# ScalarE instead of VectorE for the residual sums of three feed-forward units

## The chip, the cores and the metric

The program runs on one core of a Trainium2 chip. The metric is the device time in microseconds (us) of one execution. TensorE is PE in the profile's tables, its weight loads are PEld, VectorE is DVE, ScalarE is ACT, GpSimd is POOL, and SP is the queue from which nearly all transfers are issued.

## What is computed

Two layers over 2048 tokens of width 640, in float32. Each layer is a sliding-window attention (32 heads of 20, eight keys two tokens apart) behind a layer norm, and a feed-forward of width 1536 behind two layer norms, each with a residual sum:

```
def _B_ref(x, w1, b1, w2, b2):
    y = _layernorm(x, axis=-1)
    h = _gelu(jnp.einsum("bsd,df->bsf", y, w1) + b1)
    return jnp.einsum("bsf,fd->bsd", h, w2) + b2

x = A_x
x = x + _A_ref(_layernorm(x, axis=-1), A_wqkv, A_wo)
x = x + _B_ref(_layernorm(x, axis=-1), B_w1, B_b1, B_w2, B_b2)
x = x + _A_ref(_layernorm(x, axis=-1), A_wqkv, A_wo)
x = x + _B_ref(_layernorm(x, axis=-1), B_w1, B_b1, B_w2, B_b2)
return x
```

The last line of `_B_ref` together with its caller is the sum that the change moves: x + b2 + h·w2.

## The kernel before, in words

The tokens are cut into four sets of 512 (four tiles of 128 tokens), and each set passes both layers, so there are eight units: 0 to 3 are the first layer, 4 to 7 the second. The residual stream x stays in SBUF for the whole run (the tile is called xf). Products are made from float16 pairs: every operand is split into a high and a low half, and three of the four half products are summed (`PASS`). Weights carry a factor WS = 64, which is taken out at the end of each sum.

A unit has five steps. (1) Layer norm, then a transposing DMA writes the transposed halves into a yT buffer (L619). (2) The query, key and value products, called QKV below (L647), are copied out of PSUM by ScalarE (L664) and spilled to DRAM, and the windows come back into the tiles qk and v. (3) Attention is nearly all VectorE: products with the queries (L731), sums over a head (L735), the soft maximum, products with the values (L757), sums over the window (L765, L769). It runs in 32 groups, four to a unit. The split of its result (L776, L779) is transposed by DMA (L792). (4) The output projection, called WO below (L804): ScalarE first writes 64·x into the PSUM bank (L816), TensorE adds its products to it without a start flag, and ScalarE copies the sum back to x divided by 64 (L821). (5) Two layer norms and the feed-forward.

The feed-forward of a unit is `mlp`. For each of twelve blocks e of 128 hidden columns there is an inner product (L859, 15 matmuls of 512 columns into one of three banks "ps"), a gelu (L865) and the copy of its high half (L868) on ScalarE, the low half on VectorE (L870), and the outer products (L880), which add up over all twelve blocks in five PSUM banks. Banks acc0 to acc3 (acc_97 to acc_100 in the orders below) hold the first 512 columns of the four tiles, and acc4 (acc_101) holds the last 128 columns of all four. The block's first weights go through three buffers c1 (c_78 to c_80), its second weights through three buffers c2 (c_81 to c_83), each loaded again from DRAM for every block of every unit (L852). GpSimd adds b2 to x ahead of time (L624), and at the unit's end five VectorE additions (from L903 and L908, through the helper at L915) add the five banks, divided by 64, to x. Unit 0 is done in two halves. Units 6 and 7 are done together by another function, `pair` (L1052, L1087 and others), which takes over the same banks and is not touched.

The order of the work is not the order of this code. Every instruction, or small group of them, is handed to a planner (`class Plan`) as an operation with an estimated duration, a priority, what it needs, what it gives and which buffers it uses. The planner simulates the five engines and the DMA queue, picks on each engine the ready operation of lowest priority number, and so fixes the order on every engine. Each engine then runs its list strictly in that order. A different operation in one place can therefore reorder everything planned after it, on every engine and in the SP queue.

Of the kernel before, what the change touches and what calls it, by code (L numbers as in the profile page):

```python
# [18 lines left out]
NF = F // P  # L19
# [4 lines left out]
WS = 64.0  # L24
# [7 lines left out]
M = 4  # L32
# [33 lines left out]
PAIRS = ("qk", "pv", "ad", "o", "sub", "at", "hlo", "yl", "xb", "ol", "wq", "lo", "lm")  # L66

TURN = 2.7

THROUGH = (("sa", 29),)  # L70
LOP = ((29, -460),)
# [218 lines left out]
def sliding_dilated_then_mlp_kernel(  # L290
# [138 lines left out]
    def mm(cols, n, prio, emit, need=(), give=(), use=()):  # L429
        plan.add("pe", cols / 2400.0 + 0.0028 * n, prio, emit, need, give, use)  # L430
# [398 lines left out]
    def mlp(at, b, t0, t1):  # L829
# [8 lines left out]
        def bank(i):  # L838
            return (f"acc{i}", at)

        def own(i):
            return i, 0, 0, BANK

        def rest(i):
            return M, i * REST, BANK, REST

        for e in range(NF):
            j = at * NF + e
            pk, hk, h32 = ("ps", ("in", j)), ("hh", j), ("h32", j)
# [25 lines left out]
            def outer(i, passes, pieces, wk=wk, hk=hk, e=e, seen=seen):  # L875
                for a, c in passes:
                    for k, c0, w0, n in pieces:
                        first = e == 0 and k not in seen
                        seen.add(k)
                        nc.tensor.matmul(accs[k][:, c0:c0 + n], tile_of(*hk)[:, a, (i - t0) * P:(i - t0 + 1) * P],  # L880
                                         tile_of(*wk)[:, c, w0:w0 + n], start=first,
                                         stop=e == NF - 1 and (a, c) == PASS[-1], skip_group_check=True)

            if e < NF - 1:
                for i in tiles:
                    prev = [("outh", b, e - 1, i)] if e else ([("outh", b, e, i - 1)] if i > t0 else [])
                    mm(2 * D, 4, j, lambda i=i, outer=outer: outer(i, PASS[:2], [own(i), rest(i)]), need=[("hhi", j), wk, *prev],
                       give=[("outh", b, e, i)], use=[wk, hk, bank(i), last])
                    mm(D, 2, j + 0.05, lambda i=i, outer=outer: outer(i, PASS[2:], [own(i), rest(i)]),
                       need=[("hlo", j), ("outh", b, e, i)], give=[("out", b, e, i)], use=[wk, hk, bank(i), last])  # L890
# [6 lines left out]
        for i in tiles:  # L897
# [5 lines left out]
        dve(REST * (t1 - t0), -991, lambda: add(  # L903
            x[u][:, t0:t1, BANK:], accs[M][:, t0 * REST:t1 * REST].rearrange("p (t c) -> p t c", c=REST)),
            need=[("out", b, NF - 1, ("rest", at)), *[("xb", b, i) for i in tiles]], give=[("xr", la + 1, u, i) for i in tiles],
            use=[last])
        for i in tiles:
            dve(BANK, -990, lambda i=i: add(x[u][:, i, :BANK], accs[i]),  # L908
                need=[("out", b, NF - 1, i), ("xb", b, i)], give=[("x", la + 1, u, i)], use=[bank(i)])
            if la == 1:  # L910
                dma(P * D * 4 / 1e3, -900, lambda i=i: nc.sync.dma_start(rows(out, u)[:, i], x[u][:, i]),
                    need=[("x", la + 1, u, i), ("xr", la + 1, u, i)], give=[("done", u, i)])

    def add(xs, ps, plus=None):
        nc.vector.scalar_tensor_tensor(xs, ps, 1.0 / WS, xs if plus is None else plus, op0=OP.mult, op1=OP.add)  # L915
# [411 lines left out]
```

## Time and profile before

| | us |
|---|---|
| three runs | 1149.23, 1156.69, 1147.42 |
| their median | 1149.23 |
| profiled execution, its own time | 1146.92 |
| its span, first to last instruction | 1145.1 |
| what lies around the span | 1.8 |
| TensorE busy in the span | 1136.8 |
| VectorE busy | 1052.4 |
| ScalarE busy | 594.2 |
| GpSimd busy | 113.9 |

The profile is one execution. "Busy" counts the time in which an engine has an instruction under way; matmuls overlap each other, so the mean time of one is longer than the step from one to the next, and the step is busy time over count where they run back to back. The page's groups give line, engine, operation, tiles out<-in, shapes and count, then busy us, mean ns, and the idle time just before them with what ended it. A timeline row gives start, duration, engine, line, operation, tiles, shape and count of merged instructions.

### The profile page before, as it was taken

How to read it: one execution, taken by the hardware profiler on the slowest of the kernel's cores; microseconds unless marked ns; L12 is line 12 of the kernel's file. 1: busy time of each engine (PE TensorE's matmuls, PEld its weight loads, DVE VectorE, ACT ScalarE, POOL GpSimd, SP SyncE). 2: the span in 40 equal slices, each digit the busy share in tenths (PEclk: the TensorE clock that was granted, in tenths of full speed). 3: DMA queues.
4: the chain of work that ended last, by engine and by line, in shares of the span. 5: the costliest groups of instructions: out<-in, count | busy, mean ns of one | idle time of the engine just before them, and what ended most of it. 6: DMA issues, size and time to landing. Idle time of an engine off the chain costs nothing.

```text
span 1145.1 us, 17492 instructions
## 1 busy us (share of the span) xinstructions
PE 1136.8 (99%) x6834; PEld 629.1 (55%) x6834; DVE 1052.4 (92%) x1043; ACT 594.2 (52%) x1103; POOL 113.9 (10%) x94
## 2 busy tenths in 40 slices
PE   9999999999999999999999999999999999999998
PEld 6444446576655465546555645555455555554476
DVE  7899999999999999999999999999999995858972
ACT  6385436636355276725627653378257334747630
POOL 1010000111101111120112011012110000000000
PEclk9999999999999999999999999999999999999999
DMA  9999999988786478567755775577666656885101
GB/s 304 307 296 269 303 347 251 300 290 243 224 247 193 132 217 220 166 200 202 187 201 181 194 180 193 179 189 196 184 201 172 202 176 162 183 251 150 43 24 69
DMA packets 239790, 235.47 MB, mean 206 GB/s; under 512 B 139020, under 2 KB 195164, under 8 KB 239708
## 3 DMA queue, kind: packets, MB, share of 16 engines
q1 hardware_dynamic: 239708, 234.36, 69.8%
q8 instruction: 53, 0.87, 0.3%
q14 instruction: 29, 0.24, 0.1%
HBM read 157.55 MB, written 44.78 MB: 177 GB/s over the span
## 4 chain that ended last, share of the span: by engine, by line
PE 89%; DVE 6%; issue 2%; DMA 2%; ACT 1%; POOL 0%; SPq 0%; POOLq 0%; DVEq 0%; ACTq 0%
PE ps L647 31%; PE acc L880 19%; PE ps L859 18%; PE ps L804 10%; PE acc L1052 4%; PE ps L1087 4%; PE ps L1052 2%; DVE pr L757 1%; DVE pr L731 1%; DVE pr L765 1%; DMA qk<-spill 1%; PE acc L1087 1%; DMA c<-mw 1%; DVE pr L984 1%; PE acc L1248 1%
## 5 line engine op out<-in xcount | busy, mean ns | idle before, releaser
L647 PE MATMUL ps<-wq,yT 128*128 128x480 f16 (+1 forms) x1950 | 391.0, 363 | 0.5 <-DMA yT<-w 0.2
L647 PEld LDWEIGHTS <-yT 128*128 128x128 f16 x1950 | 189.3, 98 | 199.1 <-DMA yT<-w 0.5
L880 PE MATMUL acc<-c,act 128*128 128x512 f16 (+1 forms) x1728 | 249.1, 299 | 0.0
L859 PE MATMUL ps<-yT,c 128*128 128x512 f16 (+1 forms) x1260 | 246.6, 349 | 1.3 <-DMA c<-mw 1.3
L880 PEld LDWEIGHTS <-act 128*128 128x128 f16 x1728 | 136.1, 98 | 106.6 <-issue 0.2
L731 DVE TENSOR_TENSOR pr<-qk 128x2560 f32<-128x2560 f32 x64 | 181.2, 2835 | 3.1 <-DMA qk<-spill 3.1
L735 DVE TENSOR_REDUCE sm<-pr 128x128 f32<-128x2560 f32 x64 | 179.4, 2806 | 0.2
L757 DVE TENSOR_TENSOR pr<-sm,v 128x2560 f32<-128x2560 f32 x64 | 179.0, 2818 | 0.4
L859 PEld LDWEIGHTS <-c 128*128 128x128 f16 x1260 | 120.2, 98 | 107.5 <-DMA c<-mw 1.6
L664 ACT ACTIVATE ev<-ps 128x480 f32<-128x480 f32 x128 | 72.4, 566 | 169.4 <-PE ps L647 155.3
L765 DVE TENSOR_TENSOR pr<-pr 128x640 f32<-128x640 f32 (+1 forms) x128 | 144.6, 1160 | 0.2
L804 PE MATMUL ps<-wo,yT 128*128 128x320 f16 x960 | 131.9, 299 | 0.0
L865 ACT ACTIVATE act<-ps,b 128x512 f32<-128x512 f32 (+1 forms) x84 | 52.3, 623 | 151.0 <-PE ps L859 141.1
L804 PEld LDWEIGHTS <-yT 128*128 128x128 f16 x960 | 93.9, 98 | 37.7 <-issue 0.2
L779 POOL TENSOR_TENSOR ohl<-w,ohl 128x640 f16<-128x640 f32 x24 | 34.3, 1431 | 472.6 <-DVE pr L731 346.8
L870 DVE TENSOR_TENSOR act<-act 128x512 f16<-128x512 f32 (+1 forms) x84 | 51.4, 614 | 10.3 <-ACT act L868 10.0
L586 POOL TENSOR_TENSOR ln<-ln,half 128x2 f32<-128x2 f32 (+1 forms) x31 | 34.7, 1125 | 225.6 <-ACT ln L583 225.5
L624 POOL TENSOR_TENSOR xf<-xf,b 128x640 f32<-128x640 f32 x24 | 39.9, 1663 | 151.8 <-DVE ohl L779 47.9
L569 ACT ACTIVATE junk<-xf 128x640 f16<-128x640 f32 x57 | 41.8, 733 | 15.6 <-DVE xf L813 8.0
L609 ACT ACTIVATE w<-xf,ln 128x640 f32<-128x640 f32 x53 | 47.1, 909 | 2.6 <-DVE w L617 2.5
L868 ACT ACTIVATE act<-act 128x512 f16<-128x512 f32 (+1 forms) x84 | 47.4, 566 | 1.8
L776 ACT ACTIVATE ohl<-w 128x640 f16<-128x640 f32 x32 | 23.5, 735 | 46.7 <-DVE w L769 46.1
(196 smaller groups left out, 1002.9 us busy)
## 6 DMA issues: line engine op xcount, KB each, us to landing
c<-mw SPq DMA_DIRECT2D x174, 320.0 KB, 3.6
spill<-ev SPq DMA_DIRECT2D x64, 480.0 KB, 3.5
qk<-spill SPq DMA_DIRECT2D x32, 880.0 KB, 5.8
v<-spill SPq DMA_DIRECT2D x32, 880.0 KB, 5.2
qk<-spill SPq DMA_DIRECT2D x32, 320.0 KB, 3.7
act<-in_B_w_dram SPq DMA_DIRECT2D x24, 320.0 KB, 5.4
mw<-c SPq DMA_DIRECT2D x24, 320.0 KB, 5.3
pr<-in_B_w_dram SPq DMA_DIRECT2D x24, 320.0 KB, 4.1
```

The costliest lines, as they stand in the source:

```text
L647: nc.tensor.matmul(ps, transposed(yk)[:, a * KD + k, t * P:(t + 1) * P], wq[:, b, k, g, i0:i1], start=first and j == 0, stop=last and j == ...
L664: act(3 * GC, -400 + n, lambda i=i, pk=pk, ek=ek: nc.scalar.activation(tile_of(*ek)[:, :, i], tile_of(*pk)[:, :3 * GC].rearrange("p (a c) ...
L731: nc.vector.tensor_mul(tile_of(*pk), w[:, HALO + m + t0:HALO + m + t0 + EH, None, :].to_broadcast([P, EH, W, GC]), windows(w, t0, [GC, W], ...
L735: dve(E, G - 0.7, lambda pk=pk, t0=t0: nc.vector.tensor_reduce(lg(t0, t0 + EH).rearrange("p t w h -> p (t w h)"), tile_of(*pk).rearrange(" ...
L757: nc.vector.tensor_mul(tile_of(*vk).rearrange("p t w (h d) -> p t (w h) d", d=DH), lg(t0, t0 + EH).rearrange("p t w h -> p t (w h)")[:, :, ...
L765: dve(EH * w * GC, G - 0.9, lambda vk=vk, w=w: nc.vector.tensor_add(tile_of(*vk)[:, :, 0:w], tile_of(*vk)[:, :, 0:w], tile_of(*vk)[:, :, w ...
L804: nc.tensor.matmul(tile_of(*pk)[:, :D // 2], transposed(yk)[:, a * KD + k, t * P:(t + 1) * P], wo[:, b, k, c * D // 2:(c + 1) * D // 2], s ...
L859: nc.tensor.matmul(tile_of(*pk)[:, :nt], tile_of(*ck)[:, a, k * P:(k + 1) * P], transposed(yk)[:, c * KD + k, t0 * P:t1 * P], start=i == 0 ...
L865: act(nt, -430, lambda pk=pk, h32=h32, e=e: nc.scalar.activation(tile_of(*h32)[:, :nt], tile_of(*pk)[:, :nt], AF.Gelu_apprx_tanh, bias=b1[ ...
L880: nc.tensor.matmul(accs[k][:, c0:c0 + n], tile_of(*hk)[:, a, (i - t0) * P:(i - t0 + 1) * P], tile_of(*wk)[:, c, w0:w0 + n], start=first, s ...
L1052: nc.tensor.matmul(tile_of(*to(i))[:, :HALF], hl()[:, a, i * P:(i + 1) * P], row(c), start=start and (a, c) == PASS[0], stop=(a, c) == PAS ...
L1087: nc.tensor.matmul(ps, wt()[:, a, w0:w0 + P], z(c), start=start and k == 0, stop=k == 3 * len(todo) - 1, skip_group_check=True)
```

## The change

For units 3, 4 and 5 (`filled = b > 2`) the five VectorE additions at the unit's end are gone. In their place ScalarE does ten things. Before the unit's first outer product it writes 64·(x + b2) into the five banks ("fills": four of 128x512, one of 128x4x128 for acc4), and the outer products then add to this with no start flag on any of them. After the last outer product ScalarE copies the five banks, divided by 64, back to x ("drains"). The first outer products (e = 0) of each tile need the fill of that tile's bank and that of acc4; the fill of acc4 comes last and needs x + b2 of all four tiles. The fill of a bank needs the bank free, which is after the drain of the unit before. Units 0 to 2 keep the VectorE additions, and units 6 and 7 are not touched.

```diff
+FILL, DRAIN = -420, -700
...
+        filled = b > 2
+        put = [("put2", b, i) for i in tiles] + [("put2", b, "rest")] if filled else []
+
+        if filled:
+            for i in tiles:
+                act(BANK, FILL, lambda i=i: nc.scalar.activation(accs[i], x[u][:, i, :BANK], AF.Copy, scale=WS),
+                    need=[("xb", b, i)] + [("out", b - 1, NF - 1, i)] * (b > 0), give=[("put2", b, i)], use=[bank(i)])
+            act(REST * M, FILL, lambda: nc.scalar.activation(
+                accs[M].rearrange("p (t c) -> p t c", c=REST), x[u][:, :, BANK:], AF.Copy, scale=WS),
+                need=[("xb", b, i) for i in tiles] + [("out", b - 1, NF - 1, ("rest", at - 1))], give=[("put2", b, "rest")], use=[last])
...
-                        first = e == 0 and k not in seen
+                        first = not filled and e == 0 and k not in seen
...
-                    mm(2 * D, 4, j, lambda i=i, outer=outer: outer(i, PASS[:2], [own(i), rest(i)]), need=[("hhi", j), wk, *prev],
+                    mm(2 * D, 4, j, lambda i=i, outer=outer: outer(i, PASS[:2], [own(i), rest(i)]), need=[("hhi", j), wk, *prev] + [("put2", b, i), ("put2", b, "rest")] * (filled and e == 0),
...
+        if filled:
+            act(REST * M, DRAIN, lambda: nc.scalar.activation(
+                x[u][:, :, BANK:], accs[M].rearrange("p (t c) -> p t c", c=REST), AF.Copy, scale=1.0 / WS),
+                need=[("out", b, NF - 1, ("rest", at))], give=[("xr", la + 1, u, i) for i in tiles], use=[last])
+        else:
+            dve(REST * (t1 - t0), -991, lambda: add(
...
         for i in tiles:
+            if filled:
+                act(BANK, DRAIN, lambda i=i: nc.scalar.activation(x[u][:, i, :BANK], accs[i], AF.Copy, scale=1.0 / WS),
+                    need=[("out", b, NF - 1, i)], give=[("x", la + 1, u, i)], use=[bank(i)])
+            else:
+                dve(BANK, -990, lambda i=i: add(x[u][:, i, :BANK], accs[i]),
+                    need=[("out", b, NF - 1, i), ("xb", b, i)], give=[("x", la + 1, u, i)], use=[bank(i)])
```

The new lines shift the line numbers: behind the top of the file by 1, from the inner products on by 12, and from `add` on by 21. So L865 before is L877 now, L804 is L805, L1087 is L1108.

The planner's order is the same on every engine up to the start of unit 3's outer products, and different after it. Ahead of the first outer products of unit 3 TensorE now has three inner products in a row where it had one. Ahead of those of units 4 and 5 it has two where it had one. Three places follow.

The first place is ScalarE's list where unit 3 ends and unit 4 begins. The rows are gelus of inner products (L865, act<-ps), copies of their high halves (L868, act<-act) and layer norm steps (L569, L573). Before:

```order
L865 ACTIVATE act<-ps_94,b_104 128x512
L868 ACTIVATE act<-act 128x512
L569 ACTIVATE junk,ln_93<-xf 128x640 x2
L573 ACTIVATE junk,ln_93<-xf,ln_93 128x640 x2
L569 ACTIVATE junk,ln_93<-xf 128x640
L865 ACTIVATE act<-ps_95,b_104 128x512
```

And now the same place, with the drains (xf<-acc) and the fills (acc<-xf):

```order
L877 ACTIVATE act<-ps_94,b_104 128x512
L916 ACTIVATE xf<-acc_101 128x4x128
L880 ACTIVATE act<-act 128x512
L926 ACTIVATE xf<-acc_97 128x512
L926 ACTIVATE xf<-acc_98 128x512
L926 ACTIVATE xf<-acc_99 128x512
L926 ACTIVATE xf<-acc_100 128x512
L853 ACTIVATE acc_97<-xf 128x512
L853 ACTIVATE acc_98<-xf 128x512
L853 ACTIVATE acc_99<-xf 128x512
L853 ACTIVATE acc_100<-xf 128x512
L855 ACTIVATE acc_101<-xf 128x512
```

Five drains and five fills now stand between two gelus, and the layer norm that reads the new x stands behind the fills instead of behind VectorE's additions.

The second place is the SP queue a little later, before the output projection of unit 5. c<-mw rows load feed-forward weights, yT<-ohl rows are the transposes that the projection reads, yT<-w rows those of a layer norm. Before:

```order
L852 DMA c_81<-mw_126 128x1280
L689 DMA v_68<-spill_138 128x1760
L792 DMA_TRANSPOSE yT_72<-ohl_75 128x10x128 x4
L619 DMA_TRANSPOSE yT_74<-w_86 128x10x128
L619 DMA_TRANSPOSE yT_74<-w_85 128x10x128
```

And now:

```order
L690 DMA v_68<-spill_138 128x1760
L864 DMA c_78<-mw_117 128x1280
L864 DMA c_81<-mw_126 128x1280
L864 DMA c_82<-mw_127 128x1280
L793 DMA_TRANSPOSE yT_72<-ohl_75 128x10x128 x4
```

The four transposes now stand behind the load into c_82, whose buffer comes free only when the second of two blocks of outer products of unit 4 is done.

The third place is TensorE's list at the output projection of unit 7. Before, at this row an inner product (L859) is followed by a block of outer products (L880):

```order
L859 LDWEIGHTS c_80
L859 MATMUL ps_96<-yT_72,c_80 128x512
L880 LDWEIGHTS act
L880 MATMUL acc_97<-c_81,act 128x512
L880 MATMUL acc_101<-c_81,act 128x128
```

And now, at the same row, the inner product is followed by the output projection:

```order
L871 LDWEIGHTS c_80
L871 MATMUL ps_94<-yT_72,c_80 128x512
L805 LDWEIGHTS yT_73
L805 MATMUL ps_95<-wo,yT_73 128x320
```

The projection of unit 7 has moved ahead by one block of outer products and one inner product.

More of the change, by code (lines that the diff above doesn't have):

```diff
@@ L901, in mlp @@
                need=[("hlo", j), ("outh", b, e, i)], give=[("out", b, e, i)], use=[wk, hk, bank(i)])
[L903 to L906, printed above, removed]
-        for i in tiles:
-            dve(BANK, -990, lambda i=i: add(x[u][:, i, :BANK], accs[i]),
-                need=[("out", b, NF - 1, i), ("xb", b, i)], give=[("x", la + 1, u, i)], use=[bank(i)])
+        if filled:
[4 more added lines that the diff above has]
+            dve(REST * (t1 - t0), -991, lambda: add(
+                x[u][:, t0:t1, BANK:], accs[M][:, t0 * REST:t1 * REST].rearrange("p (t c) -> p t c", c=REST)),
+                need=[("out", b, NF - 1, ("rest", at)), *[("xb", b, i) for i in tiles]], give=[("xr", la + 1, u, i) for i in tiles],
+                use=[last])
+        for i in tiles:
+            if filled:
[4 more added lines that the diff above has]
+                    need=[("out", b, NF - 1, i), ("xb", b, i)], give=[("x", la + 1, u, i)], use=[bank(i)])
             if la == 1:
```

## The prediction

> **What bounds the kernel now.** I read the engines' busy shares first, then TensorE's own waits, then its step per matmul, then stretches of time around and behind the change.
>
> ```profile
> PE 1136.8 (99%) x6834; PEld 629.1 (55%) x6834; DVE 1052.4 (92%) x1043; ACT 594.2 (52%) x1103; POOL 113.9 (10%) x94
> ...
> PE ps L1087 <- ACT xf L1156: 1.6, 1, 1.6
> PE acc L1248 <- POOL ident L446: 1.4, 1, 1.4
> PE ps L859 <- DMA c<-mw: 1.3, 1, 1.3
> PE ps L647 <- DMA yT<-w: 0.2, 1, 0.2
> PE acc L1052 <- ACT act L1059: 0.2, 1, 0.2
> ```
>
> TensorE is idle for 1145.1 − 1136.8 = 8.3 us of the whole span, and its five named waits are 4.7 us together. A busy TensorE need not be a fast one, so I check the step from one matmul to the next, which is busy over count where they run back to back:
>
> ```profile
> L647 PE MATMUL ps<-wq,yT 128*128 128x480 f16 x1905 | 387.7, 366 | 0.3 <-DMA yT<-w 0.2
> L804 PE MATMUL ps<-wo,yT 128*128 128x320 f16 x960 | 131.9, 299 | 0.0
> ...
> 750.40 3.42 PE L880 MATMUL acc<-c,act 128*128 128x128 f16 x24
> 753.66 3.40 PE L859 MATMUL ps<-yT,c 128*128 128x512 f16 x15
> 756.90 3.42 PE L880 MATMUL acc<-c,act 128*128 128x512 f16 x24
> 760.16 2.11 PE L859 MATMUL ps<-yT,c 128*128 128x512 f16 x9
> ```
>
> 387.7/1905 is 203.5 ns for 480 columns, 131.9/960 is 137.4 ns for 320: 0.424 and 0.429 ns a column. The timeline gives the feed-forward: a block of 24 outer matmuls (12 of 512 and 12 of 128 columns) takes 3.26 us from its start to the next one's, and 15 inner matmuls 3.24 us, both for 7680 columns: 0.424 and 0.422 ns. Four shapes have one price per column, so there are no gaps hidden in the busy time. The columns are fixed by the arithmetic, and the change leaves their number as it is.
>
> ```profile
> 600.00:1010.00 410.00, 409.97 (x2446) 219.99 (x2445) 383.75 (x355) 218.96 (x404) 47.52 (x32) 1.00 0.67 187
> 1010.00:1090.00 80.00, 78.14 (x408) 39.49 (x406) 63.42 (x104) 52.27 (x83) 0.00 (x0) 1.00 0.43 129
> 1090.00:1145.10 55.10, 51.75 (x381) 37.05 (x379) 26.60 (x54) 8.96 (x15) 0.00 (x0) 1.00 0.14 48
> ```
>
> The columns after the stretch are TensorE, its weight loads, VectorE, ScalarE and GpSimd busy, then the granted clock (1.00 throughout), DMA share and GB/s. The change begins at 610 us. From there to 1010 us TensorE has no idle time at all, between 1010 and 1090 us it has 1.86 us, and 3.35 us lie at the very end, where the last sums are added and sent, in a function that is not touched. VectorE is nearly full up to 930 us, but nobody waits for it in TensorE's list: the planner fills each of its delays with feed-forward blocks of an earlier unit.
>
> **The change part by part.** *VectorE's additions go.*
>
> ```profile
> L915 DVE SCALAR_TENSOR_TENSOR xf<-acc,xf 128x512 f32<-128x512 f32 x29 | 18.4, 682 | 1.4 <-PE acc L880 1.4
> ```
>
> A step is 18.4/29 = 0.63 us, and 15 of them are 9.5 us of VectorE: 3.2 us by 760 us, 6.3 us by 920 us, the rest at unit 5's end. None of it lies on TensorE's path, so its worth is slack for VectorE and 0 us by itself.
>
> *ScalarE's drains and fills come.* There are 30. The nearest rows are copies of 512 columns from PSUM to SBUF, and the fill of the output projection at 320 columns; the gelu and its copy, which stand between them, follow:
>
> ```profile
> L1156 ACT ACTIVATE xf<-ps 128x512 f32<-128x512 f32 x6 | 3.5, 581 | 0.0
> L1159 ACT ACTIVATE wq<-ps 128x512 f32<-128x512 f32 x4 | 2.4, 592 | 2.5 <-PE ps L1087 2.4
> L816 ACT ACTIVATE ps<-xf 128x320 f32<-128x320 f32 x56 | 23.6, 432 | 0.5
> L865 ACT ACTIVATE act<-ps,b 128x512 f32<-128x512 f32 x60 | 41.1, 684 | 123.0 <-PE ps L859 117.5 <-DVE pr L765 5.1
> L868 ACT ACTIVATE act<-act 128x512 f16<-128x512 f32 x60 | 37.6, 626 | 1.2
> ```
>
> At 0.59 us each, 30 are 17.7 us on an engine that is busy for half of the time. What counts is the chain at each unit's start. At units 4 and 5 TensorE's last outer block ends with the last tile (at 753.66 in the rows above), then two inner blocks follow, 2 × 3.24 = 6.5 us, and e = 0 starts at 760.1. In between ScalarE has at least the last drain and five fills, 6 × 0.59 = 3.5 us, and at most all ten, 5.9 us. Both fit, with 0.6 to 3.0 us to spare. With one inner block, as the order was, even the shorter chain would not have fitted into 3.24 us; the second inner block is the cover, and if it were gone the price would be 0.3 to 2.7 us a unit.
>
> At unit 3 VectorE still adds unit 2's sums, and the fills wait for them and for the last x + b2 on GpSimd:
>
> ```profile
> 610.98 3.08 DVE L915 SCALAR_TENSOR_TENSOR xf<-acc,xf 128x512 f32<-128x512 f32 x5
> ...
> 611.14 1.54 POOL L624 TENSOR_TENSOR xf<-xf,b 128x640 f32<-128x640 f32 x1 [4.40 <-DVE act L870]
> ...
> 610.79 3.40 PE L859 MATMUL ps<-yT,c 128*128 128x512 f16 x15
> ```
>
> The last addition ends at 614.06 and the last b2 at 612.68. Were the whole list of five fills, one layer norm row (0.74, below), one gelu and its copy (1.3) to run only from 614.06 on, the acc4 fill would end at 614.06 + 3.0 + 2.0 = 619.1. Three inner blocks hold TensorE until 610.79 + 3 × 3.24 = 620.5. It fits with 1.4 us at worst. The drains at unit 5's end stand before the pair's products into the same banks; the rows of inner products between them cover about 2 us, and I price this at 0 to 1 us, taking 0.
>
> *Waits behind the new work.* ScalarE's list is strict, so gelus and layer norms stand behind the ten. Only unit 3's sums are read by another layer (units 4 and 5 are outputs).
>
> ```profile
> 753.31 0.74 ACT L569 ACTIVATE junk<-xf 128x640 f16<-128x640 f32 x1 [1.36 <-DVE xf L915]
> ...
> 772.01 4.53 SPq L619 DMA_TRANSPOSE yT<-w  x3
> ...
> 786.38 3.81 PE L647 MATMUL ps<-wq,yT 128*128 128x480 f16 x18
> ```
>
> That layer norm began at 753.31 and now begins behind the fills, at 757.2 or later, some 4 us. Its transposes, issued from 772.0 on, move to 776, and the QKV products move back by one outer block to 789.6. The margin shrinks from 14.4 to about 13.6 us: 0. In the SP queue the transposes for unit 5's projection now wait for the second outer block of unit 4, which ends at 760.1 + 6.5 = 766.7. The projection begins at 773.2, one outer block after the row before (769.9), and a transpose lands 3.4 to 7.3 us after its issue, in the middle 4.3:
>
> ```profile
> 769.89 16.65 PE L804 MATMUL ps<-wo,yT 128*128 128x320 f16 x120
> DMA to landing us min/median/max: 3.4/4.3/7.3
> ```
>
> That is 771.0 for the first tile, 774.0 at the latest: 0 to 0.8 us, and I take 0.
>
> The tightest place is unit 7's projection. It moves ahead by one outer and one inner block, 6.5 us, from 961.7 to 955.2:
>
> ```profile
> 953.08 0.82 DVE L779 TENSOR_TENSOR ohl<-w,ohl 128x640 f16<-128x640 f32 x1 [0.80 <-ACT ohl L776]
> ...
> 954.51 9.06 SPq L792 DMA_TRANSPOSE yT<-ohl  x4
> ...
> 955.24 3.42 PE L880 MATMUL acc<-c,act 128*128 128x512 f16 x24
> 958.50 3.40 PE L859 MATMUL ps<-yT,c 128*128 128x512 f16 x15
> 961.74 4.51 PE L804 MATMUL ps<-wo,yT 128*128 128x320 f16 x32
> ```
>
> Its transposes were issued at 954.5, 7.2 us ahead. VectorE is to be 6.3 us earlier there, so issue comes at 948.2, 7.0 us ahead. If VectorE's relief arrives in full the wait is 0 to 0.3 us; if none of it arrives, 6.5 us.
>
> ```profile
> 630.00:780.00 150.00, 150.00 (x883) 80.57 (x882) 148.18 (x124) 81.17 (x152) 17.84 (x12) 1.00 0.71 189
> 780.00:850.00 70.00, 69.97 (x380) 36.02 (x379) 69.24 (x56) 31.22 (x64) 13.39 (x8) 1.00 0.68 191
> 850.00:930.00 80.00, 80.00 (x502) 43.78 (x500) 79.01 (x66) 41.26 (x73) 4.11 (x4) 1.00 0.60 185
> ```
>
> VectorE idles for 3.6 us in these 300 us, so a shorter list ends earlier by nearly as much; I take 0.5, near the first end.
>
> *The tail.* The pair's order is new too. Before, it holds one wait of 1.6 us for ScalarE's L1156 and 1.86 us idle in all. The new order may lose it or hold others: −1.9 to +2 us, and I take −0.5, since the pair's layer norm comes earlier.
>
> The sum is 0 + 0 + 0.5 − 0.5 = 0: a span of 1145.1 us and, with the 1.8 us around it, 1146.9 us for the execution, rounded to 1147. The median of the runs shown, 1149.2, stands 2.3 us above that execution.
>
> **The rivals.** *Unit 7's projection waits.* VectorE's relief is eaten by the layer norm's low halves, which now come later from ScalarE. The price is up to 6.5 us, typically 4 with the tail: 1151. For it speaks the small margin, against it that VectorE is full and takes any work early.
>
> *The fills become the bound (slower).* If ScalarE reaches the drains late in each filled unit, because an Exp with its two table loads stands in the chain, the outer products of e = 0 wait:
>
> ```profile
> L746 ACT ACT_TABLE_LOAD x20 | 25.7, 1283 | 0.4
> L746 ACT ACTIVATE sm<-sm 128x256 f32<-128x256 f32 x32 | 13.3, 415 | 27.9 <-DVE sm L744 27.6
> ```
>
> The Exp and a table load on either side of it are 3 us, and with a gelu and copy (1.3 us) a chain of 5.9 grows to 10.2, against a cover of 6.5: 3.7 us a unit, 11 us for three, and 1158. It decides from a chain of 10.3 us on. Against it: the order has the Exp behind the fills.
>
> *VectorE is the true bound (faster).* If its additions delayed attention one for one up to the end, 9.5 us would go: 1137. VectorE's 92% speaks for it, the 410 us without a gap in TensorE against it. The Trainium skill, Perfetto Trace Analysis, section Identifying the Most-Contended Engine, holds matmul busy time a poor measure of headroom and names weight-load busy time instead; by that rule TensorE stands at 55%, VectorE is the most-contended engine, and the time would be the 1137 of this rival. This trace disagrees: the constant 0.42 to 0.43 ns a column shows a full TensorE.
>
> **How the numbers follow.** About 1% (11.5 us) is what a measurement of this kernel can tell from no change. My forecast, no more than 4 us from 1147, gets 0.74; the late projection 0.12; the fills as the bound 0.09, of which 0.08 lie beyond 1%; VectorE as the bound 0.05, of which 0.02 lie beyond it. So: faster by over 1% 0.02, within 1% 0.90, slower 0.08. The range goes from 1142 (the tail's 1.9 us gone and a quick execution) to 1154 (the late projection at its full 6.5 us); it leaves out the fills, VectorE and the ends of the others, some 0.17.
>
> **What would show it.** Right: TensorE still without idle time between 600 and 1010 us, VectorE's busy time 9.5 us less, ScalarE's some 16 more, L853 and L855 done before e = 0 starts, WO of unit 7 near 955 us. Wrong: an idle time of TensorE before L892 that a fill ends (the fills), before L805 that a transpose ends (unit 7), new waits of L1108, or a span shorter by more than 4 us, which would mean that TensorE's busy time was not its floor.

## The result, and the profile after

The changed kernel takes 1146.16 us (median of 22 runs, 1144.6 to 1147.8), the kernel before 1149.97 us (22 runs, 1146.7 to 1161.0). The ratio is 0.9956, interval 0.994 to 0.9972: the same by the prediction's measure of 1%, and 3.8 us less in the median. The forecast was 1147.0 in a range of 1142 to 1154. Three executions of this record ran at a granted clock of 0.26 to 0.85 (4321.6, 2018.0 and 1322.5 us) and stand in no median or count below. The two profiled executions differ by much less than the medians: 1146.3 us with a span of 1144.5, against 1146.92 with 1145.1. So most of the gain is not to be found by laying those two traces side by side. What changed most is the spread: in the kernel before six of 22 executions lay above 1155, in the changed one none lies above 1148.

The page after, its first line, and TensorE's waits (engine, tile, line, what it waited for: us in all, times, longest):

```profile
PE 1136.8 (99%) x6834; PEld 629.0 (55%) x6834; DVE 1041.5 (91%) x1028; ACT 609.3 (53%) x1133; POOL 115.3 (10%) x94
...
PE acc L1269 <- POOL ident L447: 1.3, 1, 1.3
PE acc L892 <- DVE xf L936: 1.3, 1, 1.3
PE ps L648 <- ACT xf L822: 0.9, 1, 0.9
PE ps L1108 <- DVE wq L1182: 0.3, 1, 0.3
PE ps L648 <- DMA yT<-w: 0.2, 1, 0.2
```

TensorE's busy time is the same to the tenth, VectorE has 10.9 us less, ScalarE 15.1 us more. Gone is the wait of 1.6 us for L1156 at the pair's start; new are the third line and, with 0.3 us, the fourth. (The second line, at 266 to 268 us, lies ahead of the change.) The three stretches of the prediction, columns as there:

```profile
600.00:1010.00 410.00, 409.09 (x2436) 219.01 (x2434) 378.06 (x350) 234.38 (x433) 49.41 (x32) 1.00 0.67 189
1010.00:1090.00 80.00, 79.66 (x426) 40.94 (x424) 60.10 (x99) 53.98 (x88) 0.00 (x0) 1.00 0.40 120
1090.00:1144.50 54.50, 51.13 (x377) 36.55 (x374) 24.79 (x51) 6.56 (x11) 0.00 (x0) 1.00 0.14 49
```

TensorE loses 0.9 us in the stretch of the change, where it lost nothing, and gains 1.5 us in the pair (0.34 idle, 1.86 before). That accounts for the 0.6 between the two executions. The places on which the prediction rested, from the timeline after (start, duration, engine and line):

```profile
756.81 0.59 ACT L855 ACTIVATE acc<-xf 128x512 f32<-128x512 f32 x1
...
760.51 6.68 PE L892 MATMUL acc<-c,act 128*128 128x512 f16 x48
...
773.53 2.74 PE L805 MATMUL ps<-wo,yT 128*128 128x320 f16 x19
...
948.82 8.92 SPq L793 DMA_TRANSPOSE yT<-ohl  x4
...
956.50 5.73 PE L805 MATMUL ps<-wo,yT 128*128 128x320 f16 x41
```

Unit 4's last fill ends at 757.4, 3.1 us before e = 0 needs it. The projections of units 5 and 7 begin at 773.5 and 956.5 and wait for nothing.

The new wait of 0.9 us is small, but it holds the key to the rest. This is what the engines do ahead of it, in the timeline after:

```profile
779.24 5.54 DVE L758 TENSOR_TENSOR pr<-sm,v 128x2560 f32<-128x2560 f32 x2
784.71 0.81 DVE L618 TENSOR_TENSOR w<-w,w 128x640 f16<-128x640 f32 x1
785.45 2.88 DVE L766 TENSOR_TENSOR pr<-pr 128x1280 f32<-128x1280 f32 x2
791.51 0.82 DVE L618 TENSOR_TENSOR w<-w,w 128x640 f16<-128x640 f32 x1 [3.19 <-ACT w L616]
...
782.27 7.32 POOL L780 TENSOR_TENSOR ohl<-w,ohl 128x640 f16<-128x640 f32 x1 [12.17 <-ACT w L616]
...
789.62 0.92 ACT L610 ACTIVATE w<-xf,ln 128x640 f32<-128x640 f32 x1 [4.00 <-POOL ohl L780]
790.44 0.41 ACT L822 ACTIVATE xf<-ps 128x320 f32<-128x320 f32 x1
790.91 9.27 PE L648 MATMUL ps<-wq,yT 128*128 128x480 f16 x45 [0.91 <-ACT xf L822]
```

GpSimd's subtraction L780 takes 1.4 us elsewhere in this trace. Here it takes 7.3. VectorE goes from one operation with two inputs in SBUF straight to the next, from 779.2 to 788.3, and GpSimd's ends 1.3 us after that row does. ScalarE's list is strict: its L610 needs the buffer that L780 reads, waits 4.0 us for it, and behind L610 stands the copy that frees a PSUM bank for TensorE. So VectorE can hold TensorE up without TensorE ever waiting for VectorE by name: through GpSimd, which is busy for 10% of the time, and ScalarE's list.

The Trainium skill, SBUF — State Buffer, section Who interferes with whom, says that a VectorE instruction with two SBUF inputs contends with a GpSimd instruction that reads SBUF, that the contention is an exclusive lock, and that the order of issue decides who blocks. This trace agrees: VectorE's row began first, and GpSimd's operation took 7.3 us against 1.4.

### The profile page after: what moved, and what is told of

The parts are those of the page before. It is cut to its first block, busy times and chain, and to the rows that moved or that the text cites. A ratio compares the mean times of both kernels' runs of the same rounds, so it can differ in the third digit from the quotient of the medians.

```text
span 1144.5 us, 17537 instructions
## 1 busy us (share of the span) xinstructions
PE 1136.8 (99%) x6834; PEld 629.0 (55%) x6834; DVE 1041.5 (91%) x1028; ACT 609.3 (53%) x1133; POOL 115.3 (10%) x94
## 4 chain that ended last, share of the span: by engine, by line
PE 91%; DVE 5%; issue 1%; ACT 1%; POOL 1%; DMA 0%; DVEq 0%; POOLq 0%; ACTq 0%
PE ps L648 34%; PE ps L871 19%; PE acc L892 19%; PE ps L805 10%; PE acc L1073 3%; PE ps L1108 3%; PE ps L1073 2%; DVE pr L1005 1%; POOL ohl L780 1%; PE acc L1269 1%; DVE pr L758 0%; DVE pr L732 0%; DVE sm L736 0%; DMA yT<-w 0%; DVE pr L766 0%
## 5 line engine op out<-in xcount | busy, mean ns | idle before, releaser
L805 PE MATMUL ps<-wo,yT 128*128 128x320 f16 x960 | 131.7, 299 | 0.0
L877 ACT ACTIVATE act<-ps,b 128x512 f32<-128x512 f32 (+1 forms) x84 | 52.3, 622 | 129.4 <-PE ps L871 125.0
L805 PEld LDWEIGHTS <-yT 128*128 128x128 f16 x960 | 93.7, 98 | 37.4
L780 POOL TENSOR_TENSOR ohl<-w,ohl 128x640 f16<-128x640 f32 x24 | 39.9, 1664 | 466.5 <-DVE pr L732 274.9
L625 POOL TENSOR_TENSOR xf<-xf,b 128x640 f32<-128x640 f32 x24 | 37.4, 1559 | 147.5 <-DVE ohl L780 44.9
L610 ACT ACTIVATE w<-xf,ln 128x640 f32<-128x640 f32 x53 | 47.5, 910 | 7.3 <-POOL ohl L780 4.0
L618 DVE TENSOR_TENSOR w<-w,w 128x640 f16<-128x640 f32 x56 | 44.9, 817 | 4.6 <-ACT w L616 4.4
L880 ACT ACTIVATE act<-act 128x512 f16<-128x512 f32 (+1 forms) x84 | 47.3, 565 | 3.3 <-PE acc L892 1.5
```

Source lines behind the costliest of these rows:

```text
L805: nc.tensor.matmul(tile_of(*pk)[:, :D // 2], transposed(yk)[:, a * KD + k, t * P:(t + 1) * P], wo[:, b, k, c * D // 2:(c + 1) * D // 2], s ...
L877: act(nt, -430, lambda pk=pk, h32=h32, e=e: nc.scalar.activation(tile_of(*h32)[:, :nt], tile_of(*pk)[:, :nt], AF.Gelu_apprx_tanh, bias=b1[ ...
```

## Experiments

The first four runs were made before the place just shown was understood; their theories are "relief" (VectorE's shorter list removes the spread), "order" (the new order does), "tail" (the pair's wait) and "late inputs" (what VectorE makes for the output projections comes just in time). From the fifth run on the theory is the lock: GpSimd's small operations wait for VectorE's rows, and ScalarE and then TensorE wait for them. Its rival is late inputs: a longer VectorE list reaches TensorE by itself.

**1. The kernel before, profiled again.** No edit.

> The kernel before, unchanged, once more with a profile: its runs scatter from 1146.7 to 1161.0 us, those after the change only from 1144.6 to 1147.8, and the profile of before was a quick execution. If the late-input theory holds (the inputs that VectorE makes for the output projections come just in time), an execution of 1150 us or more shows 3 us or more of idle TensorE before L804 at units 5 to 7, near 770, 848 or 962 us. If the tail theory holds (the pair's new order), the idle time lies in L1087 or L1052 after 1010 us. If it lies before 610 us, neither holds, since both kernels have the same order there.

Measured: 1149.26 us, span 1147.5; the 25 executions of before beside it fall into two groups, 18 from 1146.9 to 1150.8 and 7 from 1153.9 to 1155.8. This profile is 2.4 us longer than the first one of the same kernel. The timelines of the two at one place, the first profile of before and then this one:

```profile
789.37 3.98 POOL L624 TENSOR_TENSOR xf<-xf,b 128x640 f32<-128x640 f32 x1 [5.33 <-DVE pr L765]
793.32 1.28 POOL L586 TENSOR_TENSOR ln<-ln,half 128x2 f32<-128x2 f32 x1
```

```profile
789.75 9.07 POOL L624 TENSOR_TENSOR xf<-xf,b 128x640 f32<-128x640 f32 x1 [5.33 <-DVE pr L765]
798.78 0.70 POOL L586 TENSOR_TENSOR ln<-ln,half 128x2 f32<-128x2 f32 x1
...
799.51 0.48 ACT L591 ACTIVATE ln<-ln 128x1 f32<-128x1 f32 x2 [7.21 <-POOL ln L586]
```

And from TensorE's waits in this run:

```profile
PE ps L647 <- ACT ev L664: 1.6, 1, 1.6
```

The new idle time lies neither where late inputs would put it (3 us or more before L804) nor in the pair. Of the 2.4 us, 1.6 are this wait, and 0.7 are two waits of L804 for its fills. The same addition of b2 (1.54 us where nothing disturbs it) took 4.0 us in one execution and 9.1 in the other. Behind it on GpSimd stands the power −1/2 of a layer norm, behind that ScalarE, which waits 7.2 us, and behind that the copy L664, for which TensorE waits 1.6 us. The instruction lists are identical: the difference is whether GpSimd gets in between two operations of VectorE (in the first profile it did, at 791.9) or has to wait until VectorE stops.

**2. VectorE's work put back into the new order.** Nothing of the result changes; 15 reductions of 512 columns into a scrap column are added on VectorE where ScalarE's drains stand, unknown to the planner. The lists of the other engines stay those of the changed kernel.

```diff
-                act(BANK, DRAIN, lambda i=i: nc.scalar.activation(x[u][:, i, :BANK], accs[i], ...),
+                act(BANK, DRAIN, lambda i=i: (nc.vector.tensor_reduce(scrap, b2[:, :BANK], axis=AX.X, op=OP.add),
+                                              nc.scalar.activation(x[u][:, i, :BANK], accs[i], ...)),
```

> The order of the kernel after on TensorE, ScalarE and GpSimd, but VectorE gets 15 operations of about 0.6 us (a sum over 512 columns of b2 into one unused column) at the places of the drains, unknown to the planner. Relief theory (VectorE's shorter list is what takes the waits away): back to the median of before, 1149 to 1150 us, with runs above 1152. Order theory (the relief is worth nothing, the new order with inner products in stock is): 1146 us, all runs below 1149, ratio 0.995 to 0.997.

Measured: 1149.93 us, nine executions from 1147.4 to 1152.1, ratio to before 0.9997 (0.9978 to 1.0016). The new order without the relief gains nothing. The profile of this kernel that can be read is run 7's.

**3 and 4. One unit only.** `filled = b == 5` and `filled = b == 3` in place of `filled = b > 2`.

> The change in unit 5 alone, so that the order is that of before up to about 911 us and only unit 5's start and the pair's tail are new. Tail theory: 1146 us with a narrow scatter, ratio about 0.996. Late-input theory (waits at units 5 and 6, 770 to 870 us): most of the scatter of before stays, median 1148 to 1150.

> The change in unit 3 alone. VectorE is relieved of 3.2 us at 760 us and keeps its additions in units 4 and 5; the order is new from 610 us on. Late-input theory: 1146 us with a narrow scatter, ratio about 0.996, since the places at units 5 and 6 have their slack. Relief summed over three units: a third of the gain, median 1148 to 1149.

Measured: unit 5 only 1147.7 us, ratio 0.9969 (0.9944 to 0.9995), ten executions from 1145.2 to 1155.7; unit 3 only 1149.04, ratio 0.9989 (0.997 to 1.0007), from 1147.3 to 1150.9. Both lose the wait at the pair's start. With unit 5 only the scatter stays, so the tail is not its cause; with unit 3 only none is above 1151, but the median is not the 1146 that late inputs asked for. The profile with unit 5 only has a span of 1154.0, and up to 911 us all its lists are those of before, so it shows what one of the long executions looks like. TensorE's longest wait in it, then its timeline:

```profile
PE ps L805 <- ACT ps L817: 5.0, 2, 4.8
```

```profile
757.58 5.55 DVE L758 TENSOR_TENSOR pr<-sm,v 128x2560 f32<-128x2560 f32 x2
763.04 0.69 DVE L882 TENSOR_TENSOR act<-act 128x512 f16<-128x512 f32 x1
763.65 4.36 DVE L766 TENSOR_TENSOR pr<-pr 128x1280 f32<-128x1280 f32 x4
767.92 0.49 DVE L770 TENSOR_TENSOR w<-pr 128x320 f32<-128x320 f32 x1
...
761.12 7.86 POOL L587 TENSOR_TENSOR ln<-ln,half 128x2 f32<-128x2 f32 x1 [36.70 <-ACT ln L584]
...
769.01 0.48 ACT L592 ACTIVATE ln<-ln 128x1 f32<-128x1 f32 x2 [4.77 <-POOL ln L587]
...
775.30 0.78 ACT L817 ACTIVATE ps<-xf 128x320 f32<-128x320 f32 x2
```

A power of 128x2 numbers lasts 7.9 us, from 761.1 to 769.0, through VectorE's whole row, which ends at 768.4. ScalarE stands for 4.8 us, and the fills of unit 5's projection (L817), which stand in its list behind the layer norm, come that much later; TensorE waits for them.

The wait costs more than its length, for TensorE's granted clock is 0.50 behind it (columns as in the stretches of the prediction):

```profile
776.00:780.00 4.00, 4.00 (x17) 2.27 (x16) 4.00 (x4) 2.31 (x6) 0.00 (x0) 0.50 0.86 162
```

TensorE is busy for 1140.2 us in this profile, with the same 6834 matmuls; the ten profiles at a clock of 1.00 have 1136.2 to 1137.7. Runs 6 and 7 below show a clock of 0.50 as well, from 793.8 to 796 us, behind waits of 3.3 and 3.5 us; behind the 1.6 us of run 1 it is 1.00. The mean granted clock is known for 101 executions of the kernel before: it is below 1.000 in all 28 at 1153 us or above, and in 9 of the other 73. This fits long executions that hold a long wait of TensorE and a slower clock behind it, though only this one profile shows such an execution.

**5. VectorE waits for the two powers, in the kernel before.** A copy of one column behind each of the two powers near 758 and 762 us makes VectorE stand still until GpSimd is done.

```diff
+                nc.gpsimd.tensor_tensor(col(2)[:, t0:t1], col(2)[:, t0:t1], half[:, t0:t1], op=OP.pow)
+                if name == ("a", 7):
+                    nc.vector.tensor_copy(scrap, col(2)[:, t0:t0 + 1])
```

> The kernel before, with two tiny VectorE copies (one column into a scrap tile), each placed right behind the place where the plan puts one of the two GpSimd powers of unit 7's first layer norm (near 758 and 762 us). A copy reads what the power writes, so VectorE stands still until GpSimd has done its power. Nothing else changes; TensorE's, ScalarE's and GpSimd's lists are those of before. The theory of the lock: GpSimd's power (0.69 us when nothing disturbs it) cannot begin while VectorE goes from one operation with two SBUF inputs straight to the next; it took 2.6 us in two executions and 7.9 us in a long one, and ScalarE's strict list, with the fills of unit 5's output projection behind, stood for 4.8 us. Then the group of executions at 1153 us and above (7 of 25 for the kernel before) must be gone, no run above 1152, and the median comes to 1147 to 1149, ratio 0.996 to 0.999, although VectorE has up to 2 us more to wait. The theory of late inputs (VectorE's own list is too long, GpSimd does not matter): the group stays at about a quarter of the runs, and the median is 1150 to 1152, for VectorE is 1 to 2 us later.

Measured: 1149.3 us, twelve executions from 1147.5 to 1152.6, ratio 0.999 (0.997 to 1.001); of the 28 of before beside it eight are above 1153. The long group is gone, as the lock has it; the highest run is 0.6 and the median 0.3 above the bounds that I gave, and the median did not move beyond the interval, so there is a second source of spread.

**6. The same copy behind fifteen powers, in the changed kernel.** The edit of run 5 with `if n >= 4`.

> The changed kernel with the same tiny copy behind all of the powers of the layer norms from unit 4's first norm on (15 copies): VectorE waits for each, up to 0.7 us and the way there and back, some 10 us in all, as much as the change took off VectorE. The theory of the lock: the changed kernel loses little to the lock already, and a power that never waits makes up for what VectorE waits: 1145 to 1147.5, no run above 1148.5. The theory of late inputs: VectorE's relief is given back, and the time goes where the runs with the fifteen reductions went: 1149 to 1151.

Measured: 1148.76 us, 1145.2 to 1151.3, ratio 0.9979 (0.9954 to 1.0003). A miss for the lock as I had put it, which was about powers alone (1145 to 1147.5 expected); the median lies just below the 1149 to 1151 of late inputs. The profile has a wait of TensorE for L827 of 3.3 us at 790, at the place of the 0.9 us above: GpSimd's subtraction lasts 7.3 us as in the changed kernel, but it begins 2.9 us later (785.18 against 782.27).

**7. The kernel of run 2 again.**

> The changed kernel's order with fifteen VectorE reductions put back (the kernel of the second run), run again for a profile that can be read. The time is 1147 to 1152 again. The theory of the lock: where TensorE stands still beyond what it does in the changed kernel, a GpSimd power or addition of more than 3 us stands at the head of the chain. The theory of late inputs: the gaps of TensorE follow VectorE's own results (a transpose that is issued late, a low half that comes late), with GpSimd's powers at 0.7 to 2 us.

Measured: 1151.44 us, 1150.2 to 1152.2, ratio 1.0007 (0.9984 to 1.003). TensorE's longest wait, then the timeline:

```profile
PE ps L649 <- ACT xf L823: 3.5, 1, 3.5
```

```profile
785.24 7.31 POOL L781 TENSOR_TENSOR ohl<-w,ohl 128x640 f16<-128x640 f32 x1 [13.59 <-DVE pr L759]
...
792.58 0.92 ACT L611 ACTIVATE w<-xf,ln 128x640 f32<-128x640 f32 x1 [6.38 <-POOL ohl L781]
```

All is as in the changed kernel, and 3.0 us later: 785.24 against 782.27 for GpSimd, 792.58 against 789.62 for ScalarE. TensorE's own work is only 0.4 us later (a wait at L806), so its wait here grows by 2.6 us, from 0.9 to 3.5. The five reductions put back by then (about 3 us of VectorE) reach TensorE by this chain, nearly one for one. The spans differ by 4.4 us (1148.9 against 1144.5): another 1.0 is TensorE's busy time, 1137.8 us, which the clock behind the wait may explain, though run 4 has 1137.7 at a clock of 1.00.

**8 and 9. That one subtraction on VectorE.** Group 24 is unit 6's first. The plan is left alone; VectorE does the subtraction (0.8 us) where the plan puts GpSimd's. Run 8 makes the edit in the kernel of runs 2 and 7, run 9 in the changed kernel.

```diff
-            pool(ASIDE, -300 + G, lambda: lo(nc.gpsimd), ...
+            pool(ASIDE, -300 + G, lambda: lo(nc.vector if G == 24 else nc.gpsimd), ...
```

> The kernel of the second and seventh runs (the changed order, fifteen VectorE reductions put back), with one operation moved: the low half of the attention output of unit 6's first column group (L780, 1.4 us on GpSimd when nothing disturbs it) is computed by VectorE (0.8 us) at the place where the plan puts GpSimd's, between two rows of two-input operations. VectorE has 0.8 us more to do than in the seventh run. The theory of the lock: in the seventh run this one operation lasted 7.3 us on GpSimd, until VectorE's row ended, ScalarE waited 6.4 us for it and TensorE 3.5 us at 790; with it on VectorE the wait at 790 is under 1 us and the time 1147 to 1149. The theory of late inputs (a longer VectorE list reaches TensorE by itself, the lock does not matter): it stays at 1150 to 1152.5.

> The changed kernel with the same single operation moved from GpSimd to VectorE; a version that may beat both kernels. The theory of the lock: the wait of 0.9 us at 789.7 goes, ScalarE does not stand for 4.0 us there, and the median is 1145 to 1146, not above the changed kernel's 1146.2. The theory of late inputs: VectorE is 0.8 us later, and the time is 1146 to 1147.5.

Measured: run 8 1147.2 us, 1146.0 to 1148.0, ratio 0.9961 (0.9938 to 0.9983); run 9 1145.19 us, nine executions from 1144.7 to 1146.0, ratio 0.9946 (0.9923 to 0.9969). TensorE's waits in run 8, where the one at 790 is gone and one of 1.5 us for unit 7's transposes takes part of its place, and then in run 9:

```profile
PE ps L806 <- DMA yT<-ohl: 1.5, 1, 1.5
PE acc L1270 <- POOL ident L448: 1.4, 1, 1.4
PE acc L893 <- DVE xf L937: 1.2, 1, 1.2
PE ps L806 <- ACT ps L818: 0.4, 1, 0.4
PE ps L1109 <- DVE wq L1183: 0.3, 1, 0.3
```

```profile
PE acc L1269 <- POOL ident L447: 1.3, 1, 1.3
PE acc L892 <- DVE xf L936: 1.3, 1, 1.3
PE ps L1108 <- DVE wq L1182: 0.3, 1, 0.3
```

In run 8 VectorE has more to do than in runs 2 and 7, and the time is 2.7 us less than run 2's median and 4.2 less than run 7's, with whose executions (from 1150.2 on) its own do not overlap. The three were not timed side by side; their ratios to the kernel before, timed beside each, are 0.9961 against 0.9997 and 1.0007. That VectorE is late is not the main cost; that it keeps GpSimd out while it is late is. Run 9 is the fastest of all: its median is 1.0 below the changed kernel's, though the two were not timed side by side.

**10 and 11. The places of before cured.** Run 10 is run 5 with the addition of b2 of unit 5's first tile (the 4.0 and 9.1 us of run 1) on VectorE. Run 11 has also the copy behind the powers of unit 5's second layer norm.

```diff
-                if name == ("a", 7):
+                if name in (("a", 7), ("b", 5)):
...
-                pool(ASIDE, -200 + n, lambda t=t: nc.gpsimd.tensor_add(x[u][:, t], x[u][:, t], b2),
+                pool(ASIDE, -200 + n, lambda t=t: (nc.vector if (n, t) == (5, 0) else nc.gpsimd).tensor_add(x[u][:, t], x[u][:, t], b2),
```

> The kernel before with its two places of the lock cured and nothing of the change: VectorE waits for the two powers near 758 and 762 us as in the fifth run, and the one addition of b2 to x that lasted 4.0 us in one execution and 9.1 us in another (GpSimd, at 789, unit 5's first tile) is done by VectorE at the place where the plan puts it. The theory of the lock: the scatter of before comes from these two places; no run above 1151, median 1147 to 1148.2. What is left against the changed kernel is the 1.6 us wait at the pair's start, which the change's order loses. The theory of late inputs: as the fifth run, 1149 to 1150.5.

> The tenth run's kernel (before, with VectorE waiting for the powers near 758 and 762 us and doing the addition of b2 at 789 itself), with the third place of the lock cured too: VectorE also waits for the two powers of unit 5's second layer norm, of which the later one, at 790.3, lasted 7.4 us in the tenth run's profile. The theory of the lock: the tenth run's upper half (six of twelve executions between 1149.4 and 1152.1) goes, no run above 1149, and the median is 1146.8 to 1147.8; the 1.6 us wait at the pair's start stays. The theory of late inputs: VectorE waits still longer, and the two halves stay, 1148.5 to 1150.

Measured: run 10 1148.56 us, 1146.6 to 1152.1, ratio 0.9975 (0.9953 to 0.9997), six executions below 1148 and six above 1149. Median and highest run are 0.4 and 1.1 above the bounds that I gave: two places were not all. Its profile shows the next one in line, now that the addition is out of the way:

```profile
790.30 7.43 POOL L588 TENSOR_TENSOR ln<-ln,half 128x2 f32<-128x2 f32 x1 [6.52 <-ACT ln L584]
...
797.77 0.48 ACT L596 ACTIVATE ln<-ln 128x1 f32<-128x1 f32 x2 [5.96 <-POOL ln L588]
```

Run 11, with that cured as well: 1147.85 us, 1146.8 to 1149.5, ratio 0.9988 (0.9974 to 1.0001). Median and highest run are 0.05 and 0.5 above the bounds that I gave; the upper half of run 10 is gone but for its lower end. The ratio's interval holds 1, for the executions of before beside it had only two above 1153, so the size of this gain is not settled by it alone. TensorE's longest wait is now the pair's:

```profile
PE ps L1092 <- ACT xf L1161: 1.6, 1, 1.6
```

Beside it stand two waits, 1.3 us together, for the fills of unit 5's projection, behind the protected power, which still took 3.2 us in this profile. Run 11 less the pair's wait would be 1146.2 us, the changed kernel's median; no run shows that sum, and the changed kernel has a wait of 0.9 us that run 11 has not.

**12. The relief alone.** All lists as before; the fifteen additions of units 3 to 5 take 2 columns of each tile's share of a bank instead of all 512 or 128. The rest of these units' feed-forward sums is left out of the output.

```diff
+        def few(n):
+            return 2 if 3 <= b <= 5 else n
...
-            dve(BANK, -990, lambda i=i: add(x[u][:, i, :BANK], accs[i]),
+            dve(BANK, -990, lambda i=i: add(x[u][:, i, :few(BANK)], accs[i][:, :few(BANK)]),
```

> The kernel before, with all five engines' lists as they are, and VectorE's fifteen additions of units 3 to 5 made on 2 columns of each bank instead of 512 or 4 x 128: the sums of these units' feed-forward are left out of the output but for those columns. It is the change's relief of VectorE (some 8 us) without its new order and without ScalarE's work. If the relief by itself made the change's gain, the time is 1146.5 to 1147.5, with no run above 1149 (the wait at the pair's start stays). By the theory of the lock the relief counts only through where GpSimd's operations fall against VectorE's rows, and in the order of before VectorE's row and the layer norm's power both move up together: executions above 1153 remain, if fewer, and the median is 1147.5 to 1149.5.

Measured: 1148.85 us, 1147.0 to 1150.6, ratio 0.9993 (0.9978 to 1.0007). The relief without the order gains nothing in the median either. None of the twelve is above 1151, but beside it only four of 22 of before are, and two above 1153, so this run says little about the long group. Its profile still has the addition of b2 at 789.8 at 4.0 us, a power at 655.3 at 5.4 us, and the pair's wait of 1.6.

**Over all runs.** Of 123 executions of the kernel before, 34 are at 1153 us or above (from 11 of 26 beside run 10 to 2 of 22 beside runs 11 and 12). With the power at 758 to 762 us protected (runs 5, 10 and 11) none of 36 is. With the lists of before up to that place (run 3) two of ten are.

**A place that no run tests.** The profiles show one collision more, with two outcomes in the order of before. GpSimd's power near 654 us, in the first profile of before and then in run 1, there with the VectorE row at which it got in:

```profile
654.49 1.83 POOL L586 TENSOR_TENSOR ln<-ln,half 128x2 f32<-128x2 f32 x1 [30.75 <-ACT ln L583]
```

```profile
653.93 5.35 POOL L586 TENSOR_TENSOR ln<-ln,half 128x2 f32<-128x2 f32 x1 [30.43 <-ACT ln L583]
658.65 0.62 DVE L743 TENSOR_REDUCE sm<-sm 128x32 f32<-128x256 f32 x1
```

It took 1.8 to 2.0 us in the profiles of before and of runs 5 and 10 (executions of 1146.9, 1147.9 and 1147.5 us), and 5.2 to 5.4 in those of runs 1, 3, 11 and 12 (1149.3, 1155.7, 1148.5 and 1148.3). In these four VectorE then stands for 1.8 us, between 662.7 and 666.0 us, waiting for ScalarE, and the power near 760 begins at 759.6 to 761.1 instead of 758.4 to 758.7. In the changed order (the profiles of after and of runs 4 and 7 to 9) it took 1.9 us each time. TensorE does not wait at this place itself. So part of the spread may begin here; it stays open, for no run changes this place alone.

## Why the prediction was right, and where its reasons were not

*TensorE's fixed work.* Right: 1136.8 us busy before and after, and nothing that was tried went below 1144.6 us. It is fixed only at a clock of 1.00 (1140.2 us in run 3).

*ScalarE's drains and fills, 0.* Right. The spare time was 3.1 us at units 4 and 5, just above the upper end of my 0.6 to 3.0 us, and 3.5 us at unit 3 (the last fill ends at 617.3, e = 0 begins at 620.9), where I had 1.4 us at worst. The rival of the fills as the bound did not come about. With unit 5 alone it began to show: TensorE waited 0.8 us for a fill (L853) there.

*Unit 5's projection, 0; unit 7's, +0.5.* They began at 773.5 and 956.5 (773.2 and 955.2 predicted) and did not wait. The transposes of unit 7 were issued at 948.8 (948.2 predicted). The +0.5 was not needed. In run 8, with VectorE's work back, this wait did appear, 1.5 us long; so the rival was a real one, and VectorE's relief keeps it away: run 9, the same kernel without that work, has no such wait.

*The tail, −0.5.* The sign was right, the size too small: 1.5 us of idle time went. Every profile in a changed order (runs 3, 4 and 6 to 9) is without the wait, every one in the order of before (runs 1, 5 and 10 to 12) has it.

*Layer norm and QKV, 0.* Wrong by 0.9 us in the profile, and with it the sign "TensorE still without idle time between 600 and 1010 us". I looked at the transposes that feed the QKV products, and they were in time. The products were to begin at 789.6 and began at 790.9. They waited for a PSUM bank, whose read-out stands in ScalarE's list behind a step that GpSimd holds up.

*VectorE's additions, "its worth is slack for VectorE and 0 us by itself".* This is the step that failed in its reason. Taken alone, in the old order, it is 0 within the interval (run 12). But in the new order the same slack is worth 3.8 to 5.3 us (1146.2 against 1149.9 and 1151.4 in runs 2 and 7). I took "nobody waits for VectorE in TensorE's list" for "VectorE is off the path". The path goes through GpSimd, busy for 10% of the time, for which my sum has no term but the last b2 of unit 3. The rival that VectorE is the true bound is wrong too: run 8 has more VectorE work than run 7 and is 4.2 us faster, and run 12 takes 8.1 us off VectorE (1044.3 us busy) for nothing. With it goes the reading by weight-load time alone, which gave 1137. The Trainium skill, Perfetto Trace Analysis, section Identifying the Most-Contended Engine, names MFU (the matmul work done, as a share of what the peak rate would do) beside weight-load busy time; the prediction left that half out. It set the rule aside by the constant price per column, and run 12 bears that out.

*The median.* My sum was made against an execution of 1146.9 that was among the quickest of its kernel, and I left the 2.3 us to the median standing as scatter. Most of the result lies in it: of the 3.8 us, 0.6 separate the two profiled executions (1.5 of the pair less 0.9 of the new wait), and 3.2 are the loss of the long executions and of part of the spread below them. Without its six long executions the median of before is 1148.9 us: about 1.1 us goes with the long group, and some 2.1 us lie in the spread below it. So it is in part luck that 1147.0 is only 0.8 above the measured median: the sum started from an execution 3 us quicker than its kernel's median, and the change then took 3.8 us off that median, for the most part for reasons that the sum did not hold. That the long group comes from the power near 760 us is shown (34 of 123 against 0 of 36, and the profile of run 3). That the spread between 1147 and 1151 comes from the addition and the power near 790 is supported by runs 1, 10 and 11, within intervals that are about as wide as the effect. Why the changed order is so much less exposed is only argued: its layer norm begins after the fills, so that the power near 760 falls at 763.5, on a reduction of VectorE's, and takes 0.7 us in the profiles of the changed kernel and of run 9 (3.6 in runs 7 and 8), and the power near 654 takes 1.9 us in the five profiles named above.

## What to carry to other kernels

When executions of one kernel differ by more than the effect that you look for, the spread is itself a cost with a cause: compare two profiles of the same kernel, and look for the instruction whose duration differs. Read the shortest, the middle and the longest duration of a line, not its mean, as this row of run 3 gives them for GpSimd's powers in ns:

```profile
L587 POOL TENSOR_TENSOR ln<-ln,half x31: 549/702/7858, 13.7 to 995.1; 128x2 f32<-128x2 f32 x26, 128x1 f32<-128x1 f32 x5
```

An engine's share of busy time says nothing of what stands behind it in another engine's strict list. And before more VectorE work is taken off, try to move the one small GpSimd operation that collides with it (run 9).

## What was not expected of the hardware

A GpSimd operation that has to wait for VectorE does not always get in at the next boundary between two VectorE instructions. The power in run 3 stood through the boundaries at 763.0, 763.7 and those within and behind the row of four, and began only when VectorE stopped; so did the addition in run 1, the subtraction in the changed kernel and in run 7, and the power in run 10. With the same lists, the addition of the first profile of before did get in, and then it was VectorE that stood: its next operation (L617) took 2.15 us instead of 0.81.

```profile
791.88 2.15 DVE L617 TENSOR_TENSOR w<-w,w 128x640 f16<-128x640 f32 x1
```

So the price of the same collision is 1.3 us of VectorE in one execution, and up to 7.5 us of GpSimd, with ScalarE and TensorE behind it, in the next. A VectorE reduction, which has one input, did not keep GpSimd out: the power at 763.5 in the changed kernel began 0.2 us into one and took 0.7 us. The long powers near 654 us in runs 1, 3, 11 and 12 and the one of 3.6 us in run 7 point the same way: less the 0.69 us of an undisturbed power, each began within 0.1 us of the start of a reduction (658.6 against 658.65 in run 1, 766.2 against 766.27 in run 7).
